# A fused recurrent attention and feed-forward kernel: a new written-out order and a new choice of engines for all its steps

## The chip, the cores and the metric

The kernel runs on one core of one Trainium2 chip. A core has five engines with queues of their own: TensorE (PE; its weight loads are shown as PEld), VectorE (DVE), ScalarE (ACT), GpSimd (POOL) and SyncE (SP), which here only issues DMA transfers. The metric is the device time of one execution in microseconds. Before the change, three runs took 184.97, 185.97 and 186.15, a median of 185.97.

## What is computed

Inputs are q, k, v and the logits of a gate f, each 4 x 8 x 768 x 48 (batch, heads, sequence, head width), and two weight matrices, 384 x 2048 and 2048 x 384. For each batch and head a 48 x 48 state runs along the sequence:

```python
f = 1.0 / (1.0 + np.exp(-f_logit))
for t in range(S):
    state = f[:, :, t, :, None] * state + np.einsum('bhd,bhe->bhde', k[:, :, t], v[:, :, t])
    y[:, :, t] = np.einsum('bhd,bhde->bhe', q[:, :, t], state)
# y as x: 3072 tokens x 384
h = x @ w_in
g = h * np.cos(h)
out = g @ w_out
```

## The kernel before

**Tiling.** The sequence is worked in 12 pairs of 128-position chunks: pair n is batch n // 3 and the 256 positions from 256 x (n % 3). Within a chunk the recurrence is written as masked attention; between chunks a state is carried. The feed-forward part works in 13 units of tokens (`UNITS`), the first two of 128 tokens (pair 0), the others of 256, one pair each: unit m is pair m - 1 from m = 2 on.

**Steps.** `describe` (L169 on) builds a graph of named steps. A name has a kind and a number, often a part: `sc5.1` is the scores of pair 5, half 1 (heads 4 to 7). The kinds, by engine:

- loads on SP: `f`, `k`, `q`, `v` of a pair (in halves for pairs 0 and 1), `w0.i` and `w1.i` for quarters of the two weight matrices, `out` for results;
- `zf` (L265): a matmul of a zero tile on TensorE, 128 x 512, whose result nobody reads; `ZEROS` says how many there are. `zsz`, `zqk`, `zvt`, `zsp` set buffers to zero;
- gate: `ex`, `ln`, `fx`, `fy` (ScalarE), `ad` (GpSimd), `cum` (TensorE, L375 and L381, running sums), `eb` and `ei` (ScalarE, decays up to a position and their inverse);
- `qa`, `ka`, `qm`, `km`: q and k times gate and decay, mostly on GpSimd; `vb` and the four `vt` copies of v; `wc` casts a quarter of the weights to bf16;
- `tq`, `tk`: transposes on TensorE (L436) for pairs 0 to 4, with the copy `qkt` out of PSUM; for pairs 5 to 11 `tq` is a transposing DMA of SP (L425);
- `sc` scores (L457), `am` their mask (VectorE), `ps` state updates (L480), `st` and `sz` carry and decay the state (VectorE; the last digit of the name tells the lower or the upper 64 partitions);
- `y` and `yi` (L532): output of a pair from within and from before the chunk, `xe` the copy to bf16;
- feed-forward: `h` (L580; six matmuls, or twelve in the first two units), `co` cosine (ScalarE), `g` the product (VectorE), `o` (L596; four matmuls, four such steps for 128 tokens), `ot` copy, `out`.

On TensorE, `h` and `o` use the whole array with 256 or 384 columns; `sc`, `ps`, `y` and `yi` are many small matmuls on parts of it.

**What sets the order.** There is no scheduler at build time. `ORDER` is a text in which every step stands with its engine (T, S, V, G, Y for PE, ACT, DVE, POOL, SP) and, where it writes a new buffer, the buffer's number. `emit` (L621) reads it from the front and gives each step's instructions to that engine. So the order of the words is the order of every queue, and a step that waits holds all that stand behind it on its engine. Semaphore waits follow from what steps read and write, and from buffers: a step that takes buffer 0 of a pool waits until the last reader of what was in it is done. Who made the text, a planner outside the kernel, isn't in the file; only its outcome is. A step may go to one of several engines, as listed at its `G.step`.

```python
    for word in ORDER.split():
        name, how = word.split(":")
        plan.append((G.steps[name], LETTER[how[0]], [int(x) for x in how[1:].split(",") if x]))
```

Of the kernel before, what the change touches and what calls it, by code (L numbers as in the profile page):

```python
# [15 lines left out]
B, H, S, D = 4, 8, 768, 48  # L16
# [16 lines left out]
ZEROS = 56  # L33
# [3 lines left out]
zsz.1:G zqk.1:G zsp.0:G f0.1:S0 f1.1:Y1 f0.0:S ex0.1:S f1.0:Y k0.1:Y0 q0.1:Y0 ex0.0:S k0.0:Y q0.0:Y  # L37
f3:Y2 ln0.1:S0 k1.1:Y1 k1.0:Y q1.0:Y1 fx0.1:S ex1.0:S ln0.0:S zf0:T0 zf1:T0 zf2:T0 zf3:T0 zf4:T0
zf5:T0 zf6:T0 zf7:T0 zf8:T0 zf9:T0 zf10:T0 zf11:T0 zf12:T0 zf13:T0 cum0.1:T0 zf14:T1 zf15:T1 zf16:T1
zf17:T1 cum0.0:T1 ei0.1:S0 fx0.0:S ei0.0:S eb0.0:S0 eb0.1:S ln1.0:S0 ex1.1:S ln1.1:S zf18:T2 zf19:T2  # L40
zf20:T2 zf21:T2 zf22:T2 zf23:T2 cum1.0:T0 ei1.0:S1 fx1.0:S zf24:T2 zf25:T2 zf26:T2 cum1.1:T1 zvt.1:G
zqk.0:G ka0.1:V zsz.3:V km0.1:V0 ka0.0:G qa0.1:V km0.0:V zsz.2:V qa0.0:V qm0.0:V ka1.0:G v0:Y0
vb0:G0 v1:Y1 f2:Y0 ex3:S eb1.0:S1 ln3:S0 fx1.1:S q1.1:Y zsp.2:V qm0.1:V w0.1:Y0 k3:Y0 tk0.1:T2
tk0.0:T3 tq0.0:T zf27:T4 tq0.1:T qkt0.0:V0 qa1.0:V qm1.0:V1 km1.0:V qkt0.1:V1 ad3:G0 vt0.3:S1
ei1.1:S zf28:T4 zf29:T4 zf30:T4 zf31:T4 zf32:T4 zf33:T4 zf34:T4 zf35:T4 zf36:T4 zf37:T4 zf38:T4
zf39:T4 zf40:T4 zf41:T4 zf42:T4 sc0.1:T2 eb1.1:S fy3:S fx3:S ex2:S ps0.0:T0,4 sc0.0:T6 am0.1:V0
am0.0:V1 w0.0:Y1 tk1.0:T5 cum3:T1 tq1.0:T qkt1.0:V2 ps0.1:T sz0.00:V2 sz0.01:V st0.10:V st0.11:V
q3:Y0 vt0.1:S ln2:S0 vt0.2:G zvt.0:G vt0.0:G vb1:G1 ka1.1:G km1.1:G ad2:G0 zf43:T2 zf44:T2 zf45:T2
# [141 lines left out]
def describe(nc, cpool, ppool, q, k, v, f_logit, moe_w_in, moe_w_out, out):  # L190
# [3 lines left out]
    def tl(shape, dt, name):  # L194
        return cpool.tile(shape, dt, name=name)
# [523 lines left out]
```

## Time and profile before

| | |
|---|---|
| profiled execution, us | 185.23 |
| its span, us | 183.5 |
| three runs, us | 184.97, 185.97, 186.15 |
| instructions | 5820 |
| busy: PE / PEld / DVE / ACT / POOL, us | 175.5 / 125.6 / 138.8 / 132.3 / 105.3 |
| matmuls | 2466, of which 56 are of zeros (15.8 us busy) |
| DMA | 33.92 MB, mean 185 GB/s |

The profile is of one execution on the chip. Times count from the start of its span. A row such as "54.12 0.53 issue" in the chain of waits is start, length and what the time was spent on; the chain is followed back from the last instruction to what released it. "issue" is time in which an engine waited for nothing that the profile shows. A row of groups has line, engine, operation, tiles written and read, count, then busy us, mean ns of one, and idle time of the engine before them with what ended it. A row of windows has the stretch, its length, and for each engine its busy time and in brackets the number of instructions, then the clock granted to TensorE, the busy share of the DMA engines and GB/s. Busy times of matmuls overlap a little, so prices of TensorE's steps are best taken from start to start in the chain.

### The profile page before, as it was taken

The page shows a single profiled execution, that of the slowest core. Times are in us where ns is not written, and L with a number is a line of the kernel's source. Part 1 is how long each engine was busy: PE and PEld are TensorE (multiplying, and loading weights), DVE is VectorE, ACT ScalarE, POOL GpSimd, SP SyncE. Part 2 cuts the span into 40 slices and gives each one's busy share as a digit, 9 for nine tenths or more (in the row PEclk, how much of TensorE's full clock was granted, in tenths as well). Part 3 has the DMA queues.
Part 4 walks back from the last instruction along what each step waited for, and adds up shares of the span by engine and source line. Part 5 has one row for each costly group of instructions (what it writes and reads, how often), then busy time and mean ns, then how long its engine had stood idle before and what let it go on. Part 6 is the DMA issues. An engine that isn't in the chain of part 4 may idle for free.

```text
span 183.5 us, 5820 instructions
## 1 busy us (share of the span) xinstructions
PE 175.5 (96%) x2466; PEld 125.6 (68%) x2466; DVE 138.8 (76%) x206; ACT 132.3 (72%) x192; POOL 105.3 (57%) x134
## 2 busy tenths in 40 slices
PE   7999889999989999999999999999999999999991
PEld 2455567976568866778667786667887677778650
DVE  5287998997578999995998887967797984573900
ACT  2786999874689999989999699767684436424520
POOL 7118599993779998999354896594996000000000
PEclk9999999999999999999999999999999999999999
DMA  5999999899997929979799949789743700030043
GB/s 141 261 261 284 345 345 338 264 282 310 249 265 163 297 42 194 302 81 217 101 230 270 259 95 212 166 240 255 154 78 106 151 4 4 0 129 4 0 172 129
DMA packets 72281, 33.92 MB, mean 185 GB/s; under 512 B 65344, under 2 KB 70720, under 8 KB 72256
## 3 DMA queue, kind: packets, MB, share of 16 engines
q1 hardware_dynamic: 71056, 33.07, 73.5%
q10 hardware_dynamic: 1200, 0.49, 1.1%
q8 instruction: 19, 0.31, 0.8%
q14 instruction: 6, 0.05, 0.1%
HBM read 25.17 MB, written 4.72 MB: 163 GB/s over the span
## 4 chain that ended last, share of the span: by engine, by line
PE 66%; DMA 8%; POOL 7%; ACT 7%; SPq 7%; issue 3%; DVE 0%; POOLq 0%; ACTq 0%
PE ps L580 29%; PE ps L596 28%; DMA f<-in_f_logit_dram 5%; POOL qk L405 4%; PE ps L532 4%; SPq L297 4%; DMA out_dram<-ot 2%; SPq L425 2%; PE ps L457 2%; PE ps L436 2%; POOL vt L198 1%; PE ps L480 1%; ACT vt L198 1%; POOL q L342 1%; ACT ls L334 1%
## 5 line engine op out<-in xcount | busy, mean ns | idle before, releaser
L562 DVE TENSOR_TENSOR g<-ps,co 128x1024 bf16<-128x1024 f32 x48 | 60.9, 1311 | 11.9 <-ACT co L585 11.7
L596 PE MATMUL ps<-w_out_bf,g 128*128 128x384 bf16 x384 | 69.1, 326 | 0.0
L580 PE MATMUL ps<-x,w_in_bf 128*128 128x256 bf16 (+1 forms) x624 | 68.3, 264 | 0.7 <-issue 0.3
L585 ACT ACTIVATE co<-ps,halfpi 128x1024 bf16<-128x1024 f32 x48 | 52.4, 1115 | 22.2 <-PE ps L580 20.1
L580 PEld LDWEIGHTS <-w_in_bf 128*128 128x128 bf16 x624 | 56.7, 98 | 10.3 <-issue 1.2
L596 PEld LDWEIGHTS <-g 128*128 128x128 bf16 x384 | 36.1, 98 | 21.1
L462 DVE TENSOR_TENSOR am<-ps,pmask 128x1024 bf16<-128x1024 f32 x24 | 28.8, 1219 | 5.2 <-PE ps L457 5.0
L405 POOL TENSOR_TENSOR qk<-k,bi 128x384 bf16<-128x384 f32 x21 | 20.9, 1003 | 0.9
L405 POOL TENSOR_TENSOR qk<-q,b 128x384 bf16<-128x384 f32 x20 | 19.8, 1003 | 0.7
L352 POOL TENSOR_TENSOR k<-k,f 128x384 f32<-128x384 f32 (+1 forms) x13 | 11.9, 916 | 12.8 <-ACT f L348 5.2
L265 PE MATMUL ps<-zero 128*128 128x512 bf16 x56 | 15.8, 428 | 1.5 <-DVE zero L204 1.2
L364 POOL TENSOR_TENSOR sp<-ls 128x384 bf16<-128x384 f32 x10 | 10.0, 1001 | 11.0 <-ACT ls L334 10.4
L198 POOL COPY vt<-vb 64x384 bf16<-64x384 bf16 x29 | 14.5, 503 | 2.5 <-issue 1.1
L504 DVE TENSOR_TENSOR sz<-ps,b 64x192 bf16<-64x192 f32 x40 | 14.0, 353 | 2.4 <-PE ps L480 1.1
L330 ACT ACTIVATE f<-f 128x768 f32<-128x768 f32 (+1 forms) x14 | 10.3, 747 | 6.2 <-DMA f<-in_f_logit_dram 6.2
L198 DVE COPY ot<-ps 128x384 f32<-128x384 f32 (+1 forms) x12 | 6.2, 522 | 11.3 <-PE ps L596 10.9
L198 ACT COPY ot<-ps 128x384 f32<-128x384 f32 (+1 forms) x14 | 6.2, 456 | 10.7 <-PE ps L596 7.6
L498 DVE TENSOR_TENSOR ps<-ps,sz 64x192 f32<-64x192 f32 x32 | 11.7, 366 | 1.5 <-PE ps L480 0.6
L198 ACT COPY vt<-vb 64x384 bf16<-64x384 bf16 x19 | 9.7, 508 | 2.7 <-POOL vb L198 2.5
L265 PEld LDWEIGHTS <-zero 128*128 128x128 bf16 x56 | 5.5, 107 | 8.0 <-issue 3.4
L342 POOL TENSOR_TENSOR q<-f,q 128x384 f32<-128x384 f32 x10 | 10.0, 1002 | 0.9 <-DMA q<-in_q_dram 0.9
L198 POOL CAST vb<-v 128x768 bf16<-128x768 f32 x9 | 7.4, 825 | 4.8 <-DMA v<-in_v_dram 4.8
(61 smaller groups left out, 169.2 us busy)
## 6 DMA issues: line engine op xcount, KB each, us to landing
v<-in_v_dram SPq DMA_DIRECT2D x12, 384.0 KB, 5.6
out_dram<-ot SPq DMA_DIRECT2D x22, 192.0 KB, 2.1
f<-in_f_logit_dram SPq DMA_DIRECT2D x10, 384.0 KB, 5.7
k<-in_k_dram SPq DMA_DIRECT2D x10, 384.0 KB, 6.0
q<-in_q_dram SPq DMA_DIRECT2D x10, 384.0 KB, 5.6
g<-in_moe_w_in_dram SPq DMA_DIRECT2D x4, 768.0 KB, 9.1
g<-in_moe_w_out_dram SPq DMA_DIRECT2D x4, 768.0 KB, 8.4
k<-in_k_dram SPq DMA_DIRECT2D x4, 192.0 KB, 5.1
```

The source lines that it names most:

```text
L198: (nc.scalar.copy if e == "ACT" else eng(e).tensor_copy)(out=o, in_=i)
L265: G.step(f"zf{i}", ("PE",), lambda e, dump=dump: nc.tensor.matmul(dump.ap, lhsT=zero[:, 0:128], rhs=zero, start=True, stop=True), writes=[ ...
L342: eng(e).tensor_mul(out=w.ap[:, :, 0, :], in0=t.ap[:, :, 1, :], in1=w.ap[:, :, 0, :])
L352: eng(e).tensor_mul(out=w.ap[:, :, 0, :], in0=w.ap[:, :, 0, :], in1=t.ap[:, :, 0, :])
L405: G.step(f"{nm}{n}.{u}", ("POOL", "DVE") if cut else ("POOL",), lambda e, u=u, j=j, src=src, dec=dec: eng(e).tensor_mul(out=qkp[u][j].ap[: ...
L462: G.step(f"am{n}.{u}", ("DVE",), lambda e, u=u, sc=sc: nc.vector.tensor_mul(out=am[u].ap.rearrange("p r b n -> p (r b) n"), in0=sc.ap.rear ...
L498: nc.vector.tensor_add(out=view()[s], in0=view()[s], in1=S0.ap[s, :, r, :])
L504: eng(e).tensor_mul(out=new.ap[s, :, r, :].rearrange("p (u a) n -> p u a n", u=2), in0=view()[s].rearrange("p (u a) n -> p u a n", u=2), i ...
L562: nc.vector.tensor_mul(out=o.rearrange("p b (n e) -> p b e n", e=2), in0=ph.ap.rearrange("p (b e n) -> p b e n", e=2, n=64), in1=co.ap.rea ...
L580: nc.tensor.matmul(ph.ap[:, i * T:(i + 1) * T].rearrange("p (g t) -> p g t", t=C), lhsT=w_in_bf[:, kk, f0:f0 + 128], rhs=xa[:, :, kk, :], ...
L585: G.step(f"co{m}.{j}", ("ACT",), lambda e, ph=ph, co=co: nc.scalar.activation(out=co.ap, in_=ph.ap, func=AF.Sin, bias=halfpi), reads=[ph], ...
L596: nc.tensor.matmul(po.ap[:, 0:DM], lhsT=gT.ap[:, j, i * C:(i + 1) * C], rhs=w_out_bf[:, j, :], start=(po.first and j == 4 * s), stop=(po.f ...
```

## The change

All of `ORDER` is replaced: every engine's queue has a new order, some steps are on other engines, and buffers have other numbers. `ZEROS` goes from 56 to 50. Nothing else differs; the steps, their matmuls and what each reads and writes are the same. The new text is described as planned with late blocks of TensorE's instructions, and with operations from partition 64 up running alone.

The core of it, as a diff (those parts of both texts of which the prediction speaks):

```diff
-ZEROS = 56
+ZEROS = 50
...
-zsz.1:G zqk.1:G zsp.0:G f0.1:S0 f1.1:Y1 f0.0:S ex0.1:S f1.0:Y k0.1:Y0 q0.1:Y0 ex0.0:S k0.0:Y q0.0:Y
-f3:Y2 ln0.1:S0 k1.1:Y1 k1.0:Y q1.0:Y1 fx0.1:S ex1.0:S ln0.0:S zf0:T0 zf1:T0 zf2:T0 zf3:T0 zf4:T0
...
-q3:Y0 vt0.1:S ln2:S0 vt0.2:G zvt.0:G vt0.0:G vb1:G1 ka1.1:G km1.1:G ad2:G0 zf43:T2 zf44:T2 zf45:T2
-zf46:T2 zf47:T2 zf48:T2 zf49:T2 sc1.0:T6 fx2:S ei3:S0 eb3:S2 vt1.3:S0 fy2:S vt1.2:S wc0.1:S
-sz0.11:V3 sz0.10:V ka3:G km3.0:G0 wc0.0:G qa3:G w0.3:Y2 qm3.0:G w0.2:Y3 k2:Y1 w1.0:Y0 w1.2:Y4
...
-ps3.1:T am2.1:V3 ot2:V1 st2.01:V sz3.00:V3 o1.1:T o1.3:T o3.1:T cum4:T7 sz3.01:V sz2.01:V vt3.0:G
-vt2.2:G ei4:S1 vt2.0:G eb4:S0 y3:T4,5 yi3:T k4:Y1 y2:T0,1 yi2:T ad5:G0 xe3.0:V1 xe3.1:V xe2.0:V0
-st3.11:V cum5:T7 ot3:V2 ot1:V3 sz3.11:V1 st3.10:V sz3.10:V h4.11:T4 fx4:S fx5:S xe2.1:S h3.20:T0
...
-h6.31:T co6.3:S1 y6:T2,3 yi6:T yi7:T6,7 y7:T h6.01:T4 h6.00:T xe6.0:V0 xe7.0:V2 xe6.1:V xe7.1:V
...
-ps10.1:T2,3 ps10.0:T out10:Y q10:Y0 am9.0:V0 sc9.1:T6 o13.2:T ot13:S0 y8:T4,0 yi9:T1 yi8:T am9.1:V2
-st10.00:V y9:T5 sz10.00:V1 xe9.1:V0 st10.01:V sz10.01:V st10.10:V sz10.10:V0 xe8.1:S1 xe9.0:S ka11:G
...
-out23.0:Y out18:Y out15:Y ot20:S0 out17:Y out23.1:Y out20:Y ot21:S2 out21:Y ot22.1:V3 ot22.0:S
-out22.0:S out22.1:Y
...
+qkt1.0:S0 eb1.1:S ei1.1:S ex2:S v1:Y1 am0.0:V0 am0.1:V1 sc1.0:T2 cum3:T1 qa1.1:V zsz.1:V am1.0:V2
+st0.10:V ei3:S0 ln2:S1 vb1:S1 vt0.1:G ka1.1:G qm1.1:G vt0.0:G w0.0:Y0 w0.1:Y1 zf33:T5 zf34:T5
+zf35:T5 zf36:T5 zf37:T5 zf38:T5 zf39:T5 zf40:T5 zf41:T5 zf42:T5 zf43:T5 ps1.0:T5,2 k3:Y0 q3:Y0
+km1.1:G vt1.1:S2 fx2:S fx3:S y0:T3 zf44:T6 ps1.1:T tk1.1:T6 tq1.1:T ad2:G2 xe0.0:S0 vt1.3:G vt1.0:G
+wc0.0:S zf45:T7 cum2:T3 wc0.1:G sz0.10:V1 st0.11:V sz0.11:V eb2:S0 fy3:S vt1.2:S xe0.1:S eb3:S2
+ei2:S1 fy2:S ka3:G w0.3:Y2 st1.00:V sz1.00:V3 qkt1.1:V1 zf46:T7 zf47:T7 sc1.1:T6 st1.01:V sz1.01:V
+am1.1:V0 w0.2:Y3 k2:Y1 zf48:T4 zf49:T4 yi1:T5,4 km3.0:G1 w1.0:Y0 qa3:G qm3.0:G w1.2:Y1 v2:Y1 km3.1:G
+qm3.1:G q2:Y0 wc0.2:G ka2:G km2.1:G2 km2.0:G wc1.0:G wc1.2:G vb2:G1 vt2.3:G0 vt2.0:G qa2:G vt2.1:G
+qm2.1:G qm2.0:G y1:T h0.01:T6 h0.00:T st1.10:V xe1.1:V1 st1.11:V xe1.0:V sz1.11:V1 co0.0:S0 g0.0:V4
...
+am2.1:V1 ps3.0:T6,4 ps3.1:T sc2.0:T2 am2.0:V3 sz3.00:V2 sz3.01:V q4:Y0 k4:Y1 o2.3:T o3.3:T y2:T2,3
+yi2:T st3.11:V xe2.0:V1 xe2.1:V st3.10:V cum4:T6 ei4:S1 eb4:S0 fx5:S o0.1:T o1.1:T ad5:G2 yi3:T3
+y3:T2 o3.1:T cum5:T6 o2.1:T ei5:S0 eb5:S1 ot3:S0 sz3.10:V1 xe3.0:V0 xe3.1:V sz3.11:V ot1:V1 ot2:V2
...
+eb8:S1 ex10:S ot9:S1 h6.30:T2 am7.0:V3 y6:T5,6 yi6:T y7:T0,1 yi7:T xe6.0:V1 q8:Y0 ln10:S1 ot7:S2
+h6.31:T st7.10:V xe6.1:S xe7.0:V2 sz7.10:V1 xe7.1:V st7.11:V sz7.11:V h7.31:T4 h7.30:T h6.01:T0
...
+ei11:S1 ot11:S2 eb11:S2 ot13:S0 y8:T6,7 yi8:T ps10.1:T0,1 ps10.0:T tq9.1:Y1 xe8.0:S1 sc9.1:T4
+xe8.1:S h8.01:T2 st10.00:V h8.00:T h9.30:T6 am9.1:V0 sz10.00:V1 st10.01:V sz10.01:V y9:T4,5 yi9:T
...
+ot23.1:S ot20:S0 o22.0:T7 o22.1:T o22.3:T o22.2:T out23.1:Y out23.0:Y out21:Y out20:Y ot22.0:S2
+out22.0:S ot22.1:V out22.1:Y
```

By engine, VectorE gets 185 steps for 191, ScalarE 183 for 185, GpSimd 133 for 126. Among those that move: three `qkt` copies from VectorE to ScalarE; of the casts of weights `wc0.1` and `wc1.3` go from ScalarE to GpSimd, `wc0.0` and `wc1.1` the other way; `km1.0` and `qm1.1` go from VectorE to GpSimd, and `f0.1` from ScalarE's DMA queue to SP's; 14 `vt` copies go from ScalarE to GpSimd and 5 back; 8 `ot` copies go from VectorE to ScalarE and 2 back.

130 lines of the change are left out of this document (62 added, 68 removed).

## The prediction

> **What bounds the kernel now.** I read the page first: which engine is busiest, and at which clock.
>
> ```profile
> PE 175.5 (96%) x2466; PEld 125.6 (68%) x2466; DVE 138.8 (76%) x206; ACT 132.3 (72%) x192; POOL 105.3 (57%) x134
> ...
> PEclk9999999999999999999999999999999999999999
> ...
> q8 instruction: 19, 0.31, 0.8%
> ```
>
> TensorE is the bound, at full clock, and the change takes no matmul of the reference away. So only three things can move the end: filler matmuls, time in which TensorE stands, and the start and tail around it. The last row leads to the standing. Queue q8 carries 0.31 MB in 19 pieces, 16 KB each; 2466 matmuls and 2466 weight loads are 4932 instructions, about 260 for a piece. A piece is thus a block of some 128 load-and-matmul pairs of TensorE's program. Next the windows, cut at the ends of the waits that the chain calls "issue" (waiting for nothing that the profile shows):
>
> ```profile
> 0.00:21.85 21.85, 19.85 (x223) 10.20 (x223) 14.56 (x41) 15.18 (x34) 11.11 (x24) 1.00 1.09 253
> 21.85:28.60 6.75, 6.04 (x128) 4.49 (x128) 6.46 (x13) 6.61 (x10) 5.47 (x6) 1.00 1.09 350
> 28.60:54.60 26.00, 25.49 (x383) 18.99 (x384) 21.15 (x27) 19.00 (x23) 20.52 (x23) 1.00 1.06 282
> 54.60:102.30 47.70, 47.08 (x768) 35.49 (x768) 42.47 (x62) 45.41 (x66) 37.34 (x44) 1.00 0.87 193
> 102.30:126.00 23.70, 23.36 (x383) 17.00 (x383) 19.26 (x26) 18.40 (x28) 17.90 (x22) 1.00 0.84 196
> ```
>
> The second bracket is the weight loads: 128, 384, 768, 383 between one wait and the next, that is 1, 3, 6 and 3 times 128. These waits stand at the borders of blocks: TensorE ran out of program. The chain in order of time shows them, and the prices that the rest needs:
>
> ```profile
> 28.39 0.24 issue
> ...
> 42.85 0.67 PE ps L436 x12
> ...
> 49.96 0.37 PE ps L480 x32
> ...
> 52.62 1.50 PE ps L532 x91
> 54.12 0.53 issue
> ...
> 55.33 9.19 PE ps L580 x84
> ...
> 102.01 0.34 issue
> ...
> 120.31 0.57 PE ps L457 x32
> ...
> 123.61 0.76 PE ps L596 x4
> 124.37 1.34 PE ps L532 x87
> 125.71 0.34 issue
> ...
> 147.78 0.90 PE ps L532 x56
> ...
> 171.24 8.46 PE ps L596 x52
> 179.73 0.37 DVE ot L198
> 180.12 0.32 ACT ot L198
> ```
>
> Prices: an h step is six matmuls, 9.19/84 x 6 = 0.66; an o step four, 8.46/52 x 4 = 0.65; a transpose step 0.67/3 = 0.22; a state update (ps) 0.37/2 = 0.19; scores (sc) 0.57/2 = 0.29; the y and yi of a pair 0.90 for 56 pairs of instructions. An o step behind small matmuls takes 0.76: a change of kind costs 0.1. The small matmuls run through 56 pairs in the time of eight large ones, so a block full of them is used up before the next one is there. The three later waits each stand in or just behind y/yi (L532). The last 128 pairs before them are worth 3.9, 3.9 and 2.6 us at these prices and took 4.7, 4.6 and 3.1 (counted back in the order to 49.97, 97.76 and 122.96): 0.8 + 0.7 + 0.5 = 2.0 us, of which about 0.3 is changes of kind. **Block waits after 42.85: 1.7 us.**
>
> The start is bound by loads and by two casts of weights. From the list of waits, SP's timeline and the list of issues (last number: us from issue to landing):
>
> ```profile
> POOL w_out_bf L198 <- DMA g<-in_moe_w_out_dram: 0.8, 1, 0.8
> ...
> PEld L580 <- ACT w_in_bf L198: 0.3, 1, 0.3
> ...
> PEld L580 <- POOL w_in_bf L198: 0.2, 1, 0.2
> ```
> ```profile
> 14.03 0.71 SPq L283 DMA_DIRECT2D g<-in_moe_w_in_dram  x1
> ...
> 15.36 1.39 SPq L283 DMA_DIRECT2D g<-in_moe_w_in_dram  x1
> ```
> ```profile
> g<-in_moe_w_in_dram SPq DMA_DIRECT2D x1, 768.0 KB, 7.4
> ...
> g<-in_moe_w_in_dram SPq DMA_DIRECT2D x1, 768.0 KB, 9.6
> ```
>
> The two issue rows belong to 14.03 and 15.36: w0.1 lands at 14.0 + 7.4 = 21.4, w0.0 at 15.4 + 9.6 = 25.0. TensorE's first h steps wait for their casts, although fillers (below) keep it busy meanwhile.
>
> **The change, part by part.** Fillers, 56 to 50:
>
> ```profile
> 1.19 5.47 PE L265 MATMUL ps<-zero 128*128 128x512 bf16 x14 [1.19 <-DVE zero L204]
> ...
> 12.23 3.40 PE L265 MATMUL ps<-zero 128*128 128x512 bf16 x15
> ```
>
> Six fewer at 3.40/15 = 0.22 are 1.3 us of TensorE (0.4 each in the first 5 us). They are worth that only if nothing else holds the start. So I follow what does.
>
> SP now issues w0.0 and w0.1 back to back, and k3 only behind them. Ahead of the first weight stand the same loads in both kernels (f, k, q and v of pairs 0 and 1, f of 2 and 3), so it lands at about 21.4 as before; the second comes without k3's 384 KB ahead of it: at the 282 to 350 GB/s of the windows 1.1 to 1.4 us sooner than 25.0. I take 23.5 (bounds: 22.8, if both share what w0.1 alone had, and 25.0, if nothing is gained). The cast of w0.1 moves from ScalarE to GpSimd's queue, and there it stands **in front of** all of pairs 3 and 2. GpSimd's own work before it ends earlier, near 22 by the rows below, so its extra work there (km1.0 and qm1.1 at 1.0 each) is hidden by the wait for w0.1; if that cover were gone it would cost up to 1 us.
>
> ```profile
> 22.95 1.01 POOL L352 TENSOR_TENSOR k<-k,f 128x384 f32<-128x384 f32 x1 [1.91 <-DMA k<-in_k_dram]
> ...
> 39.08 1.96 POOL L405 TENSOR_TENSOR qk<-q,b 128x384 bf16<-128x384 f32 x2
> ```
> ```profile
> L405 POOL TENSOR_TENSOR qk<-k,bi 128x384 bf16<-128x384 f32 x4 | 4.0, 1002 | 0.2
> ...
> L198 POOL CAST w_in_bf<-g 128x1536 bf16<-128x1536 f32 x2 | 2.9, 1464 | 0.1
> ```
> ```profile
> L198 POOL COPY vt<-vb 64x384 bf16<-64x384 bf16 x29 | 14.5, 503 | 2.5 <-issue 1.1
> ...
> L198 POOL CAST vb<-v 128x768 bf16<-128x768 f32 x9 | 7.4, 825 | 4.8 <-DMA v<-in_v_dram 4.8
> ```
>
> Before, GpSimd went from ka3 (22.95) to the end of qm2.0 (41.04) in 18.1 us: 12 products at 1.0, four casts at 1.46, 0.3 of starts. After, from wc0.1 to qm2.0 there are the same 12 products and four casts, and vb2 (0.83) and three vt2 copies (1.5) put ahead of qm2: 20.5 us. From 23.5 that ends at 44.0. TensorE's transpose tq2.0 reads it; before, it ran as part of the row at 42.85, with GpSimd 1.7 ahead. TensorE itself gets to it at about 43.4 (first h at 23.5 + 1.5 = 25.0, then 16 h, 7 o, 7 transposes, 2 sc and 2 ps, 17.7 at the prices, 0.3 of changes of kind and a little waiting), so **GpSimd is the later one, and the fillers' 1.3 us is hidden behind it**. So are the early block waits, and three qkt copies that move from VectorE to ScalarE (no row shows that: 0.67 by VectorE's row, 1.12 by ScalarE's 128x1024 activation; I take 1.1):
>
> ```profile
> L585 ACT ACTIVATE co<-ps,halfpi 128x1024 bf16<-128x1024 f32 x48 | 52.4, 1115 | 22.2 <-PE ps L580 20.1
> ...
> L198 DVE COPY qkt<-ps 128x1024 bf16<-128x1024 bf16 x10 | 6.6, 674 | 1.0 <-PE ps L436 1.0
> ```
>
> The first two are read by scores of pairs 0 and 1, which by my count of the queues run before 17, so well ahead of 23.5; the third has seven TensorE steps, 2.8 us, before its reader. Without cover each costs up to 1.1.
>
> From there on I count against before, where 42.85 to the last matmul at 179.73 took 136.9:
> - Behind tq2.0 the new order has 89 o steps for 91, two transpose steps and two half state updates fewer, since it did them before: -1.3 - 0.4 - 0.2 = -1.9.
> - Small matmuls are entered from large ones 18 times instead of 15: +0.3.
> - Block waits. Borders lie 128 pairs apart, counted on from 21.88 with six pairs fewer, so I know where they fall. The y and yi of pairs 2 and 3, and of 8 and 9, now have o or h steps between them, and a border no longer cuts off those of 6 and 7 behind scores. The dense blocks are worth 5.3 (y2, y3), 4.8 (y6, y7) and 3.6 (y8, y9) instead of 3.9, 3.9, 2.6; all others over 6. Taking what they took before (4.7, 4.6, 3.1) as what a block needs, none waits: -1.7 (bounds: 0 gained, to all of it).
> - Waits for data, about 0.6 over this stretch before (what is left of 136.9 over the steps' prices and the block waits), I leave: bounds 0 to 2. One that may come is wc1.1: GpSimd waited 0.8 for its load, now ScalarE does, with ex5 and ln5 of pair 5 queued behind; their reader cum5 has y2, y3 and two o steps before it.
>
> On SP, q2 now shares a buffer with q3 and holds the queue until qm3.1 has read it, near 31; w1.3, f4, v3 and w1.1 stand behind. w1.3 waits anyway until GpSimd has cast w1.0, near 37, so this costs nothing. VectorE's order changes between the lower and upper 64 partitions 50 times in both kernels: nothing. In the tail the halves of the last tile change places (ScalarE first, then VectorE): 0.37 and 0.32 one after the other either way, 0.
>
> **Sum:** 44.0 + 0.2 (the row's start against its read) + 136.9 - 1.9 + 0.3 - 1.7 = 177.8, against 179.73: -1.9. Span 181.6, this execution 185.23 - 1.9 = 183.3. The three runs have a median of 185.97, 0.7 above that execution, and a mean of 185.7; from these I say **183.8**. About 1% (1.9) is what this measurement tells from nothing, so the forecast lies on that border.
>
> [...]
>
> **The rivals.**
> 1. *The block waits stay, under another name*: they belong to the dense runs themselves, and y and yi are still there 12 times. For: all stand in or at L532. Against: the multiples of 128. Then -1.9 + 1.7 = -0.2: 185.6. That is also the case in which the plan doesn't do what it says. Chance 0.2.
> 2. *Slower: blocks come later than I take.* The block from 21.85 to 28.60 took 6.75, while loads ran at 350 GB/s. If a block needs L in the middle, the three dense ones wait 3L - 13.6 together (5.3 + 4.8 + 3.6): at L = 5.1 the 1.9 gained is gone, at 5.8 it is 1% slower, at 6.75 it is over 6.6 more, 190 and above. For: the early row. Against: 4.7, 4.6, 3.1 later, where loads run at 193 to 282. I price it at L = 6: +4.4, 188.2. Chance 0.12.
> 3. *GpSimd stands longer for w0.1*: each us later is one us, since everything of pairs 3 and 2 is behind it. If w0.1 shares the queue with k3 and q3 and lands at 25 to 26.3: +1.5 to 2.8, 185.3 to 186.6. Decides from 25.4. Chance 0.1.
> 4. *w0.1 lands before 22.8*, as its twin did in 7.4 us: TensorE's own work from h0.01 is then the gate: 182.5. Chance 0.1.
>
> Forecast: 0.48. **How the numbers follow.** Of the forecast's 0.48 some 0.36 lies beyond 1%, with all of rival 4 and a little of rival 1: faster 0.48. Slower: rival 2 and a part of rival 3, and waits of an order that no row shows: 0.17. Same: 0.35. The forecast alone would run from 182.6 to 185; rival 4's end and rival 2's beginning set the range, 181.8 to 187.2.
>
> **What would show it.** Right: wc0.1 on GpSimd idle before it until about 23.5, qm2.0 ending near 44; "issue" pieces above 0.3 in the chain gone after 45; last matmul near 177.8; tail of 3.7. Wrong: issue waits at y2, yi6, y8 or y9; a load of w0.1 after 25; ScalarE or VectorE named as releaser of TensorE for more than 1 us together after 45.

## The result, and the profile after

The changed kernel takes **185.43 us**, the median of 21 runs (183.88 to 187.94); beside it the kernel before takes 186.03 (184.91 to 186.82, also 21). The ratio is 0.9953, with a 95% interval of 0.993 to 0.9976: half a per cent faster, less than the one per cent that I had called the least this measurement tells from nothing. I had forecast 183.8, 1.2% less than before. The profiled execution took 186.14 us with a span of 184.3; its last matmul ended at 180.6, where I had 177.8. (The ratios here and below leave out runs more than 1.5% above the fastest of the same kernel: three of these 21, but six of ten of one experiment, y9_earlier, whose median says more than its ratio.)

The page of the changed kernel, the rows that answer to those of before:

```profile
PE 174.1 (94%) x2457; PEld 124.5 (68%) x2460; DVE 135.0 (73%) x200; ACT 133.0 (72%) x191; POOL 108.2 (59%) x141
...
PEclk9999999999999999999999999998899999999999
...
q8 instruction: 19, 0.31, 0.7%
```

The program still comes in 19 pieces. But the clock row, which was nines throughout before, has two eights now. The chain of waits, in order of time, around that place (line numbers are one less than before; L531 is y and yi, L579 h, L595 o):

```profile
121.19 0.95 PE ps L531 x56
...
124.82 0.39 PE ps L531 x19
125.21 1.99 issue
127.20 0.90 PE ps L531 x25
128.10 1.40 PE ps L579 x6
129.49 1.94 PE ps L595 x8
```

The first row is y8 and yi8. Then y9 begins, runs through 19 pairs, and TensorE **stands for 1.99 us** in the middle of it, waiting for nothing that the profile shows. After it an h step takes 1.40 and two o steps 1.94; they cost 0.66 and 1.30 elsewhere. The windows say why. Columns: stretch, length, busy us and count of PE, PEld, DVE, ACT and POOL, then the granted clock, DMA share, GB/s:

```profile
125.21:127.20 1.99, 0.00 (x1) 0.01 (x2) 0.36 (x1) 1.06 (x3) 1.85 (x4) 1.00 1.13 315
127.26:130.67 3.41, 3.41 (x36) 2.16 (x37) 2.24 (x3) 1.14 (x2) 1.57 (x2) 0.50 0.84 150
130.70:180.60 49.90, 49.89 (x541) 36.48 (x539) 29.26 (x28) 23.93 (x31) 8.14 (x12) 1.00 0.23 54
```

Right behind the wait the granted clock is 0.50 for 3.41 us, then 1.00 again. In the profile of the kernel before there was none: its records of the clock begin at 5.82 with 1.00 and change first at 183.31, behind the last matmul. Mean granted clocks of the 21 runs tell how often it comes: a stretch of 3.41 us at half clock in a span of 184 makes 1 - 0.5 x 3.41 / 184 = 0.991.

| granted clock | runs | span, us | time, us |
|---|---|---|---|
| 0.998 to 1.0 | 7 | 182.1 to 183.0 | 183.9 to 184.8 |
| 0.991 | 11 | 182.7 to 184.5 | 184.4 to 186.3 |
| 0.977 to 0.982 | 3 | 185.5 to 186.2 | 187.2 to 187.9 |

Of 71 runs of the kernel before that were made beside the experiments, 3 were below 0.995. So two things took the gain away: a wait of about 2 us in y9, and in two runs of three a fall of the clock.

Elsewhere this execution went as forecast. GpSimd's timeline and TensorE's (start, length, engine, line, operation; the wait before it in brackets):

```profile
23.61 1.46 POOL L197 CAST w_in_bf<-g 128x1536 bf16<-128x1536 f32 x1 [1.49 <-DMA g<-in_moe_w_in_dram]
...
44.00 1.46 POOL L197 CAST w_out_bf<-g 128x1536 bf16<-128x1536 f32 x1
```
```profile
44.12 0.40 PE L435 MATMUL ps<-ident,qk 128*128 128x128 bf16 x4
```

wc0.1 waits for its load and starts at 23.61 (forecast 23.5); the cast of GpSimd that follows qm2.0 starts at 44.00 (forecast 44.0 for qm2.0's end); TensorE's tq2.0 starts at 44.12. Counted border to border in the trace's instructions, the dense block of y2 and y3 took 5.43 and that of y6 and y7 4.73, without a wait. The third, of y8 and y9, worth 3.56 at the prices of the prediction, took 5.79.

### The profile page after: what moved, and what is told of

Read it like the earlier page. It is cut to its first block, busy times and chain, and to the rows that moved or that the text cites. A ratio compares the mean times of both kernels' runs of the same rounds, so it can differ in the third digit from the quotient of the medians.

```text
span 184.3 us, 5805 instructions
## 1 busy us (share of the span) xinstructions
PE 174.1 (94%) x2457; PEld 124.5 (68%) x2460; DVE 135.0 (73%) x200; ACT 133.0 (72%) x191; POOL 108.2 (59%) x141
## 4 chain that ended last, share of the span: by engine, by line
PE 83%; SPq 4%; DMA 4%; DVE 3%; issue 2%; ACT 2%; DVEq 0%; ACTq 0%
PE ps L579 34%; PE ps L595 34%; PE ps L531 5%; SPq L296 4%; PE ps L456 3%; DMA f<-in_f_logit_dram 3%; PE ps L479 2%; PE ps L435 1%; PE ps L264 1%; PE ps L374 1%; DMA out_dram<-ot 1%; DVE am L461 1%; DVE x L197 1%; DVE ps L497 1%; ACT co L584 1%
## 5 line engine op out<-in xcount | busy, mean ns | idle before, releaser
L595 PE MATMUL ps<-w_out_bf,g 128*128 128x384 bf16 x384 | 69.5, 328 | 0.0
L579 PE MATMUL ps<-x,w_in_bf 128*128 128x256 bf16 (+1 forms) x624 | 68.2, 266 | 0.2 <-DVE x L197 0.2
L579 PEld LDWEIGHTS <-w_in_bf 128*128 128x128 bf16 x624 | 56.5, 98 | 8.7 <-issue 0.5
L595 PEld LDWEIGHTS <-g 128*128 128x128 bf16 x384 | 36.1, 98 | 22.2 <-issue 0.7
L404 POOL TENSOR_TENSOR qk<-k,bi 128x384 bf16<-128x384 f32 x22 | 21.7, 1000 | 0.6
L197 ACT COPY ot<-ps 128x384 f32<-128x384 f32 (+1 forms) x20 | 9.0, 467 | 17.5 <-PE ps L595 13.5
L404 POOL TENSOR_TENSOR qk<-q,b 128x384 bf16<-128x384 f32 x21 | 20.8, 999 | 0.8
L197 POOL COPY vt<-vb 64x384 bf16<-64x384 bf16 x38 | 19.0, 501 | 3.4 <-issue 1.6
L264 PE MATMUL ps<-zero 128*128 128x512 bf16 x47 | 13.7, 419 | 1.3 <-DVE zero L203 1.2
L531 PE MATMUL ps<-am,vt 128*32 128x128 bf16 x384 | 8.1, 222 | 2.6 <-issue 2.0
L456 PE MATMUL ps<-qkt 48*64 48x128 bf16 (+1 forms) x304 | 9.2, 219 | 1.3 <-ACT qkt L197 1.1
L456 PEld LDWEIGHTS <-qkt 48*64 48x64 bf16 (+1 forms) x304 | 5.9, 103 | 4.7 <-ACT qkt L197 1.8
L531 PEld LDWEIGHTS <-vt 128*32 128x32 bf16 x384 | 5.9, 97 | 4.3 <-issue 4.3
```

Source lines behind the costliest of these rows:

```text
L197: (nc.scalar.copy if e == "ACT" else eng(e).tensor_copy)(out=o, in_=i)
L264: G.step(f"zf{i}", ("PE",), lambda e, dump=dump: nc.tensor.matmul(dump.ap, lhsT=zero[:, 0:128], rhs=zero, start=True, stop=True), writes=[ ...
L404: G.step(f"{nm}{n}.{u}", ("POOL", "DVE") if cut else ("POOL",), lambda e, u=u, j=j, src=src, dec=dec: eng(e).tensor_mul(out=qkp[u][j].ap[: ...
L456: nc.tensor.matmul(o[t0:t1, r, 2 * a + g, :].rearrange("p (e n) -> p e n", e=2), lhsT=wide[s, t0 // 64, :] if turned else wide[s].rearrang ...
L531: nc.tensor.matmul(py[g].ap[32 * c:32 * c + 32, C * m:C * m + C], start=(py[g].first and (g, c) not in begun), stop=(py[g].final and left[ ...
L579: nc.tensor.matmul(ph.ap[:, i * T:(i + 1) * T].rearrange("p (g t) -> p g t", t=C), lhsT=w_in_bf[:, kk, f0:f0 + 128], rhs=xa[:, :, kk, :], ...
```

## The experiments

**Theory 1**: TensorE ran out of program in y9. Its block was not there because the transfer of that block was late, and the wait made the clock fall in some runs. **Rivals**: y9 waited for data or a buffer that comes at 127.2 whatever stands ahead (theory 2); a dense run of y and yi costs 2 us wherever it stands, as rival 1 of the prediction had it (theory 3). A question inside theory 1: the trace's records of transfers put the start of this block's fetch at 124.49, 3.09 us behind the border (crossed at 121.40 in y8). Is that because of loads in the same DMA engines (1a), or is it asked for late (1b)? In the diffs below, the lines of `ORDER` are cut down to the words around the place that changes; its line breaks carry nothing.

### The same kernel again

> The changed kernel, unchanged, for a second profile. Theory 1: the wait inside y9 is there again, 1.5 to 2.5 us, at the same instruction; spans near 182.5 belong to a full granted clock (1.0), spans of 183.6 to 184.5 to a clock of 0.991, that is one stretch at half clock. If instead a run with a full clock has no wait in y9, the wait itself varies and the clock is only its consequence.

Median 184.89, ratio 0.9944 (0.99 to 0.9987). TensorE's timeline at y9:

```profile
124.70 0.46 PE L531 MATMUL ps<-am,vt 128*32 128x128 bf16 x19
126.78 0.40 PE L531 MATMUL ps<-am,vt 128*32 128x128 bf16 x13 [1.62 <-issue]
```

The wait is at the same instruction, 19 pairs into y9, and shorter (1.62); this execution had a granted clock of 0.999 and a span of 182.3. So the wait is there at a full clock too, and **the half clock is a second cost on top of it**: from the end of the wait to the last matmul it took 51.8 here (126.8 to 178.6) and 53.4 in the first profile (127.2 to 180.6), 1.6 more with the same instructions. Five of ten runs were at full clock (spans 182.1 to 182.7), five were not (183.5 to 186.1).

### y9 later, y9 earlier

```diff
-y9:T4,5 yi9:T
...
-sz10.11:V0 xe9.0:S0 fy11:S xe9.1:V g8.0:V h9.31:T o14.1:T0
+sz10.11:V3 fy11:S g8.0:V h9.31:T o14.1:T0
...
-o14.2:T h8.31:T4 h8.30:T h10.10:T2 h10.11:T h9.21:T6 h9.20:T o14.0:T
+o14.2:T o14.0:T y9:T4,5 yi9:T xe9.0:S0 xe9.1:V h8.31:T2 h8.30:T h10.10:T4 h10.11:T h9.21:T6 h9.20:T
```

> The changed kernel with y9 and yi9 moved on TensorE from behind h9.30 to behind h9.31, o14.1, o14.2 and o14.0 (o14.0 brought forward; the copies xe9 follow; the two PSUM tiles that they meet change places from there on). Nothing is left out. The 128 pairs that end in y9 are then worth 3.56 + 0.66 + 3 x 0.65 - 0.2 = about 6.0 us instead of 3.6. Theory 1 (TensorE runs out of program in y9, its block needs about 5.8 us from border to border there): no issue wait above 0.3 in y9, no stretch of half clock, last matmul near 180.6 - 4.3 = 176.3, span about 180.0, time about 181.9 in every run. Theory 2 (y9 waits for something that comes at 127.2 whatever stands before it: a buffer or data): TensorE now reaches y9 at about 127.3, so it would not wait either, but then what stands behind it (h8.31, h10.10) should take the wait: no gain in the sum over 0.5, 184.5 to 185.5. Theory 3 (dense runs cost this wherever they stand): 185.4 as before.

Median 183.67, ratio 0.9879 (0.9828 to 0.993). The wait in y9 is gone, and theories 2 and 3 with it: nothing behind y9 took it over, and y8 to yi9 cost no more than their prices. The gain was about 1 at full clock (spans 181.3 to 181.6 against 182.1 to 183.0), not the 2 that I had expected. Half of the shortfall is a new wait that the edit made: o14.0, brought forward, stood for g8.0.

```profile
128.66 0.82 PE L595 MATMUL ps<-w_out_bf,g 128*128 128x384 bf16 x4 [0.59 <-DVE g L561]
```

Three of the six runs had a lower clock all the same, and the profile shows where: at the front. From the windows of y9_later:

```profile
16.78:20.19 3.41, 3.11 (x18) 1.49 (x20) 3.27 (x7) 3.34 (x8) 2.99 (x5) 0.50 1.05 359
```

The other way:

```diff
-xe8.1:S h8.01:T2 st10.00:V h8.00:T h9.30:T6 am9.1:V0 sz10.00:V1 st10.01:V sz10.01:V y9:T4,5 yi9:T
+xe8.1:S h8.01:T2 am9.1:V0 y9:T4,5 yi9:T st10.00:V h8.00:T h9.30:T6 sz10.00:V1 st10.01:V sz10.01:V
```

> The changed kernel with y9 and yi9 moved the other way, directly behind h8.01, before h8.00 and h9.30 (am9.1 on VectorE ahead of st10.00). Nothing is left out. The dense block is then worth 2.3 us instead of 3.6. Theory 1: the border behind it is reached 1.3 us sooner and the block still comes near 127, so TensorE stands about 3.3 to 3.5 us in all (some of it for am9.1), the clock falls in every run, last matmul 1.3 to 2 later than in the changed kernel: 186 to 188. Theory 2 (data or a buffer that y9 needs at 127.2): y9 waits longer and at its first matmul, not inside it. Theory 3 (the wait is a fixed price of a dense run): same time as the changed kernel, 184.4 to 186.3.

```profile
123.63 0.63 PE L531 MATMUL ps<-am,vt 128*32 128x128 bf16 x31 [0.62 <-DVE am L461]
126.51 0.23 PE L531 MATMUL ps<-am,vt 128*32 128x128 bf16 x1 [2.25 <-issue]
```

Median **188.63**. y9 waits 0.62 for its data at its first matmul, and then 2.25 more inside, now 31 pairs in: with h8.00 and h9.30 behind it, the border falls later in y9. The block still comes at 126.5. One run of ten had a full clock (span 183.2), three had one stretch at half (185.0 to 185.4), six had two (0.982; 186.7 to 187.4). By these spans a stretch costs **about 1.9 us**; that rests on a single run at full clock, and at which of two places (below) the stretches of the other runs stood isn't known.

### What makes the block late

```diff
 def load(name, val, src, b, c, h0, h1):
...
-out=val.ap.rearrange("p h e d -> p h (e d)"),
+out=val.ap[:, 0:n_of(name, h1 - h0)].rearrange("p h e d -> p h (e d)"),
...
+def n_of(name, n):
+    return 1 if name in ("q10", "v11", "k11", "q11") else n
```

> The changed kernel with the loads q10, v11, k11 and q11, which are issued between 119.8 and 124.7, cut to one head of eight each; the other seven eighths of these loads are left out, so pairs 10 and 11 work on old data, while all instructions of the engines stay. Theory 1a (the block is late because its transfer stands behind these loads in the same DMA engines): its fetch starts within about 1 us of the border instead of 3.1 us behind it, the wait in y9 falls from 2.0 to about 0 to 0.3, the clock does not fall: span about 180 to 180.7, 182 to 182.5. Theory 1b (the lag does not come from these loads: the fetch is asked for late): wait in y9 of about 2 as before, clock at half in about two of three runs, 184.4 to 186.3.

Median 183.14, ratio 0.9847 (0.9782 to 0.9911). TensorE's timeline, y8's row and y9's (the edit adds four lines, so L535 is y):

```profile
121.35 0.63 PE L535 MATMUL ps<-am,vt 128*32 128x128 bf16 x32
...
124.92 0.63 PE L535 MATMUL ps<-am,vt 128*32 128x128 bf16 x32
```

y9's 32 matmuls stand in one row, without a wait. The fetch started 0.72 us behind the border instead of 3.09, and the block took 3.54 from border to border, just its work of 3.56: it was there when needed. The profiled span was 180.7. So the loads made the block late (1a). That "the clock does not fall" did not come: two of the four runs had 0.988, without a wait in y9. This run left work out; the next one doesn't. The wait ahead of out13 on SyncE is used to hold the loads back:

```diff
-o14.1:T0 q10:Y1 v11:Y1 out13:Y k11:Y2
+o14.1:T0 out13:Y q10:Y1 v11:Y1 k11:Y2
```

> The changed kernel with one word moved on SyncE: out13 stands ahead of q10 instead of behind v11. Its tile is ready at about 121.5, so q10 and v11, which were issued at 119.8 and 120.5, are now issued at about 121.9 and 122.6, behind the moment at which TensorE crosses the border in y8 (121.35) and its next block is asked for. Nothing is left out, and TensorE's order is that of the changed kernel. Theory 1a (the block's transfer queues behind loads that were issued just before it): the fetch starts within 1 us of the border instead of 3, the wait in y9 falls from 1.6 to 2.0 to below 0.3; span 180.7 to 181.2 at a full clock, 182.4 to 182.9, unless the later q10 makes scores of pair 11 wait (up to 1). Theory 1b (the lag of 3 us belongs to the border, not to the loads ahead): wait in y9 as before, 184.1 to 186.

Median 184.66, ratio 0.99 (0.9863 to 0.9937). SyncE's timeline, then TensorE's, of out13_first:

```profile
123.20 0.33 SPq L606 DMA_DIRECT2D out_dram<-ot  x1
123.59 0.43 SPq L296 DMA_DIRECT2D q<-in_q_dram  x1
124.11 1.29 SPq L296 DMA_DIRECT2D v<-in_v_dram  x1
```
```profile
122.82 0.63 PE L531 MATMUL ps<-am,vt 128*32 128x128 bf16 x32
...
126.39 0.63 PE L531 MATMUL ps<-am,vt 128*32 128x128 bf16 x32
```

(This execution, with a mean clock of 0.991, had lost about 1.5 us at the front by a stretch at half clock, so all times are later: ten fillers at 18.41 took 3.49, in the second profile of the changed kernel 2.32.) With the same TensorE order as the changed kernel and one word moved on another engine's queue, y9 runs through: the border in y8 is crossed at 123.04, q10 is issued at 123.59, and the block took 3.54. The DMA view of the stretch from the border on (each digit is the busy share in a fortieth of the window) for the changed kernel from 121.40 to 124.45, just before its fetch, and for out13_first from 123.04 to 125.20:

```profile
DMA  4873923679999899999999999999999999999999
...
q1 hardware_dynamic: 1994, 0.78, 105.2%
```
```profile
DMA  0000000000000000093689999998946124436799
...
q8 instruction: 1, 0.02, 3.3%
```

In the changed kernel the engines are full with q1's packets from the tenth digit on, and there is no q8 row for 3 us. In out13_first they are idle behind the border, and the fetch (q8) is the first packet that comes, at 123.96, 0.92 us behind it. So 0.7 to 0.9 from border to start is the least seen at this place but for one profile (zeros_56, below), and TensorE runs from the block about 2.6 later; a dense block of 3.5 is just enough with idle DMA engines, and 2 too little behind two loads. In ten of the eleven profiles with the whole of q10 and v11 issued ahead of the border the fetch started 2.7 to 3.7 behind it; the eleventh is that of zeros_56.

At full clock out13_first has spans of 181.4 to 181.8, about 1 less than the changed kernel. That is less than the wait of 1.6 to 2.0; two new waits are listed in its trace behind 130, an o step's for a copy out of its bank (0.6) and scores' for VectorE's g (0.2). Five of its eight runs were below 0.995.

### Borders and fillers

```diff
-ZEROS = 50
+ZEROS = 56
...
-zf40:T5 zf41:T5 zf42:T5 zf43:T5 ps1.0:T5,2
+zf40:T5 zf41:T5 zf42:T5 zf43:T5 zf44:T5 zf45:T5 zf46:T5 zf47:T5 zf48:T5 zf49:T5 ps1.0:T5,2
```

> The changed kernel with six more fillers of zeros behind zf43, 56 instead of 50, so that every later border of 128 pairs comes six pairs earlier in the order. Nothing is left out. Two questions. Where the wait stands: if it belongs to the border (theory 1), it moves from 19 matmuls into y9 to 13 matmuls into y9, about 2 us as before; if it belongs to y9's data or to y9 itself, it stays at 19 or is ahead of the first. Whether six fillers are hidden, as the prediction had it for the step from 56 to 50: then tq2.0 starts at 43.8 to 44.3 as before and the time is that of the changed kernel (184.4 at a full clock, 186 with a stretch at half); if they are not, tq2.0 starts up to 1.3 later, less the 0.3 to 0.6 that TensorE stands for vb1 there.

Median 185.36, ratio 0.991 (0.9872 to 0.9949). Rows of its timeline, tq2.0 and y9:

```profile
44.83 0.39 PE L436 MATMUL ps<-ident,qk 128*128 128x128 bf16 x4
...
126.03 0.63 PE L532 MATMUL ps<-am,vt 128*32 128x128 bf16 x32
```

Neither expectation on y9 came: in this execution there is no wait in it at all. The fetch started 0.95 us *ahead* of the border, at 121.0, between q10 (issued at 120.5) and v11 (121.2); so it was ahead of most of what stands in its way otherwise. Why six pairs do that, and four (zeros_front, below) don't, I can't tell. Six runs of ten were at 0.991; where the clock fell in them, no profile shows. On the fillers: tq2.0 starts at 44.83. Of the seven executions with 50 fillers and no early fall of the clock six have 43.8 to 44.2, but vt2_behind (below) has 44.76; the three with 54 fillers have 44.0 to 44.5. So up to 0.7 of the 1.3 us of six fillers may show here, and one execution can't tell it from that spread.

```diff
-vb2:G1 vt2.3:G0 vt2.0:G qa2:G vt2.1:G qm2.1:G qm2.0:G
+vb2:G1 qa2:G qm2.1:G qm2.0:G vt2.3:G0 vt2.0:G vt2.1:G
```

> The kernel of y9_later_g8 with three copies of GpSimd, vt2.3, vt2.0 and vt2.1, moved from ahead of qm2.1 and qm2.0 to behind them. Nothing is left out. If GpSimd's chain behind w0.1 sets the time of tq2.0, as the prediction had it, qm2.0 ends 1.5 sooner and tq2.0 starts sooner by what TensorE has in hand, 0.3 to 0.7, and the time falls by as much against y9_later_g8. If TensorE itself is the gate by now (theory 1 of the second profile: qm2.0 ended 0.6 ahead of tq2.0), qm2.0 ends near 42.0, tq2.0 stays within 0.2 of 44.2 and the time is that of y9_later_g8.

Median 185.4, ratio 0.9964 (0.9935 to 0.9994); y9_later_g8, its own base, had 184.84. From the waits, GpSimd's timeline (qm2.1 and qm2.0) and TensorE's (tq2.0):

```profile
PE ps L479 <- ACT vb L197: 0.9, 1, 0.9
```
```profile
41.29 1.96 POOL L404 TENSOR_TENSOR qk<-q,b 128x384 bf16<-128x384 f32 x2
```
```profile
44.76 0.39 PE L435 MATMUL ps<-ident,qk 128*128 128x128 bf16 x4
```

qm2.0 ends at 43.25, 1.5 ahead of tq2.0, and tq2.0 is no sooner; it is later, because ps1.0 waited 0.9 for ScalarE's cast of v1 at the front of this execution. In the profile of y9_later_g8 too qm2.0 had ended (43.61) ahead of tq2.0 (43.98). GpSimd isn't the gate in these two.

### The versions with y9 later

```diff
-sz10.00:V1 st10.01:V sz10.01:V st10.11:V co8.0:S2 sz10.11:V3 fy11:S g8.0:V
+sz10.00:V1 st10.01:V g8.0:V sz10.01:V st10.11:V sz10.11:V3 fy11:S
```

> The kernel of y9_later with g8.0 earlier on VectorE (behind st10.01, ahead of sz10.01, st10.11 and sz10.11) and co8.0 ahead of am9.1 in the text. Nothing is left out. In y9_later TensorE no longer stood in y9, but 0.6 us ahead of o14.0, for g8.0. Theory 1: this wait goes too, no idle time of TensorE above 0.2 after 35; at a full granted clock a span of 180.7 to 181.0 (the 181.3 to 181.6 of y9_later less 0.6), 182.4 to 182.8; with a stretch of half clock in the first 25 us, as y9_later had in three of six runs, 0.8 to 1.1 more. Theory 3 (a dense run costs its 2 us wherever it stands): the wait comes back in or behind y9, 183.3 to 184.4.

```profile
PE ps L595 <- DVE sz L503: 1.8, 1, 1.8
```

Median 184.84, ratio 0.9938 (0.9909 to 0.9968): **worse than y9_later**, and by my own mistake, not by theory 3. o14.1 writes the PSUM bank that sz10.01 reads. With g8.0 ahead of sz10.01, and g8.0 waiting for its cosine, TensorE stood 1.8 us for VectorE two steps sooner than it had before. The next run puts g8.0 behind sz10.01:

```diff
-sz10.00:V1 st10.01:V g8.0:V sz10.01:V st10.11:V
+sz10.00:V1 st10.01:V sz10.01:V g8.0:V st10.11:V
```

> The kernel of y9_later with g8.0 on VectorE one place group earlier: behind sz10.01, ahead of st10.11 and sz10.11, not ahead of sz10.01 as in y9_later_g8, where o14.1 stood 1.8 us for sz10.01 because it takes the PSUM bank that sz10.01 reads. Nothing is left out. Theory 1: g8.0 ends at about 126.7, as TensorE gets to o14.0; neither the 0.6 of y9_later nor the 1.8 of y9_later_g8 is left: no idle time of TensorE above 0.3 behind 35, span 180.7 to 181.0 at a full clock, 182.4 to 182.8; 0.8 to 1.1 more with an early stretch at half clock, as in three of six runs of y9_later. Theory 3 (a dense run of y and yi costs 2 us wherever it stands): 184.1 or more.

Median 183.43, ratio 0.9865 (0.9836 to 0.9893). Neither wait is left, but the spans at full clock, 181.2 to 181.6, are those of y9_later, not 0.6 less. What was saved at 128 was lost again by 152: between two borders there, 144.8 to 151.9, TensorE took 7.10, where y9_later took 6.70, and 0.2 of that is a wait of scores for VectorE's g. Half of the runs were below 0.995 again.

For that, two fillers ahead of sc1.0, where TensorE had stood 1.1 us in every profile, and two behind zf43; and buffer 1 for ot22.0, which waited for a transfer out of buffer 2 at the end. First on y9_later_g8, then on y9_later_v, then alone on the changed kernel (without the buffer):

```diff
-ZEROS = 50
+ZEROS = 54
...
-am0.0:V0 am0.1:V1 sc1.0:T2
+am0.0:V0 am0.1:V1 zf33:T2 zf34:T2 sc1.0:T2
...
-ot22.0:S2
+ot22.0:S1
```

> The kernel of y9_later_g8 with four more fillers where TensorE stood in the first 21 us (two ahead of sc1.0, where it waited 1.1, and two behind zf43, where it waited 0.6), so 54, and with buffer 1 instead of 2 for ot22.0, which waited 0.4 for a transfer out of buffer 2 to land. Nothing is left out. Theory 1 (the clock falls after TensorE has stood, the early stretch at half clock comes from the waits of 1.1, 0.6 and 0.25 there): fewer runs below 0.995 in granted clock than in y9_later_g8, tail 3.4 instead of 3.7 us, span 180.3 to 180.7 at a full clock, 182.0 to 182.4. If the early stretch does not come from these waits, it is there as often; if the fillers are not hidden, 0.4 to 0.9 is lost at the front.

Median 184.34, ratio 0.9904 (0.9866 to 0.9941), with the 1.8 of y9_later_g8 still in it, so its name is not earned. But all six runs had a granted clock of 0.998 or more, against six of twelve of y9_later_g8 at 0.997 or more.

> The kernel of y9_later_v with the four fillers and the buffer for ot22.0 of the run called best (54 fillers; ot22.0 in buffer 1). Nothing is left out. If the early stretch at half clock comes from TensorE's standing in the first 21 us, all runs have a granted clock above 0.995, as the six runs of best had; tail 3.4; span 180.3 to 180.9, 182.0 to 182.6, the fastest version. If not, half of the runs are 0.8 to 1.1 longer. A risk: the borders are four pairs earlier than in y9_later_v, and o14.0 or y9 may meet a late block again: up to 1.

Median **182.88**, ratio **0.9837 (0.9807 to 0.9867)**: the fastest version, 1.6% faster than before by the ratio, and 1.1 to 1.4% below the two medians of the changed kernel. All six runs had a clock of 0.997 or more. The expected 182.0 to 182.6 was not quite reached. The end of its chain:

```profile
169.73 7.81 PE ps L595 x48
...
177.57 0.33 ACT ot L197
...
177.92 0.36 DVE ot L197
```

The last matmul ends at 177.5, and the tail is 3.4 for 3.7. That 0.3 is the buffer's; what is left of the gain over y9_later_v goes with the fillers.

> The changed kernel with the same four fillers alone (two ahead of sc1.0, two behind zf43; 54). Nothing is left out. It tells the two places apart at which the clock can fall. If the runs of the changed kernel at 0.991 fell at the front, where TensorE stood 1.1 and 0.3 to 0.6, these fillers end them: all runs above 0.995, span 182.0 to 182.7 or less. If they fell behind the wait in y9, as in the first profile (127.3), about half of the runs stay at 0.991 with spans of 183.5 to 184.5. The borders come four pairs earlier, so the wait in y9 may be shorter, as with 56 fillers.

Median 185.29, ratio 0.9959 (0.9924 to 0.9995). Four of ten runs stayed below 0.995, and the profile is one of them. Its windows:

```profile
125.59:127.76 2.17, 0.00 (x0) 0.00 (x0) 0.38 (x2) 0.33 (x1) 2.03 (x4) 1.00 1.12 319
128.73:132.14 3.41, 3.41 (x14) 1.85 (x13) 3.31 (x5) 2.04 (x3) 1.65 (x3) 0.50 0.76 113
```

The wait in y9 is there (2.17), and the clock falls behind it. So the clock has two places at which it falls: the wait in y9, seen in two profiles, and the front, seen in those of y9_later and out13_first, whose front is that of the changed kernel. The four fillers cure the front (no fall in 12 runs of best and y9_later_vz; 13 in the 24 runs of y9_later, y9_later_v, out13_first and light_loads, which have no wait in y9 but lack these fillers), and not the fall behind y9.

## Why the prediction was wrong, by its own steps

- **Block waits: the step that failed.** "Taking what they took before (4.7, 4.6, 3.1) as what a block needs, none waits: -1.7." For y2/y3 and y6/y7 that held. For y8/y9 the need was 5.8 (5.4 to 6.0 where TensorE stood), not 3.1. The 3.1 was no property of the place but of what SyncE had issued just before. SyncE's timeline in the kernel before, where the border was crossed at 122.96 and the fetch started at 123.67, and in the changed kernel, border 121.40, fetch 124.49:

```profile
119.99 2.05 SPq L607 DMA_DIRECT2D out_dram<-ot  x4
122.09 0.45 SPq L297 DMA_DIRECT2D k<-in_k_dram  x1
123.48 0.33 SPq L607 DMA_DIRECT2D out_dram<-ot  x1
123.86 1.86 SPq L297 DMA_DIRECT2D q<-in_q_dram  x2
```
```profile
119.81 0.58 SPq L296 DMA_DIRECT2D q<-in_q_dram  x1
120.50 0.57 SPq L296 DMA_DIRECT2D v<-in_v_dram  x1
121.57 1.09 SPq L606 DMA_DIRECT2D out_dram<-ot  x1
```

  Before, the loads of q were issued at 123.86, behind the fetch; one load, k11's, stood 0.9 ahead of the border, behind four results. After, q10 and v11 were issued 1.6 and 0.9 ahead of the border, and the fetch came only behind packets of theirs. That the engines are busy does not tell the two apart. In the kernel before, from 119.9 to the start of the fetch at 123.67:

```profile
DMA  5999999999999999999999999899999996998934
...
q1 hardware_dynamic: 1669, 1.06, 100.2%
```

  They were as full, with the results, k11 and a transposing DMA, until shortly ahead of the fetch, which still came 0.7 behind the border. So a busy share alone doesn't tell how long a fetch waits; what differs is which transfers were issued, and when. I had followed SyncE's queue at the start and past q2, and had not asked what it issues beside the three dense blocks. The wait of 0.5 at this place was to go; it became 2.0 by the chain, 2.2 by the blocks (5.79 less 3.56).
- **The clock was no term of the sum at all.** I had read "full clock" from the page of before and kept it. A fall behind y9 cost 1.6 us between the two profiles of the changed kernel (about 1.9 by the spans of y9_earlier), and one at the front 0.5 to 1.6 (median spans with and without: y9_later_v 182.1 and 181.6, y9_later 182.6 and 181.5, out13_first 183.0 and 181.4); two runs of three had one or more.
- **The rest of the sum was right, and 0.9 too high.** light_loads has the same order without the wait: tq2.0 at 44.24, last matmul at 176.9, 132.7 us; my sum had 44.2 to 177.8, 133.6. The data waits of 0.6 that I had left in are gone: no wait of TensorE is listed in its trace from 44 to 178. The remaining 0.3 I can't divide between changes of kind and prices. So without the late block the forecast would have erred on the other side: 182.5 at full clock.
- **The sum, put right**: 183.3 for a full clock, less 0.9, plus the wait of 1.6 to 2.0, is 184.0 to 184.4; the seven runs at full clock have a median of 184.4. Most of the other fourteen lie above, and the median of all is 185.4.
- **The front.** The landing of w0.1, the start of wc0.1 and the time of tq2.0 were right to 0.2. That "GpSimd is the later one" was not: in the first profile and in light_loads it is by 0.1, in y9_later_v both come to tq2.0 together, and in the others TensorE gets to it 0.3 to 1.5 behind qm2.0 (1.8 to 1.9 after an early fall of the clock). What holds it, the waits name only in part: v1's cast (0.3 to 0.9 in five profiles). So the cover for the fillers' 1.3 us was not there as I had it; what taking six away was worth is not shown (at most about 0.7 by zeros_56).
- **The copies qkt on ScalarE** were hidden from the end, as said. But the first scores of pair 1 stood 1.1 for one, and it is in this neighbourhood that the clock falls at the front. A wait that costs nothing by the chain cost 0.5 to 1.6 in about half of the runs by the clock.
- **The rivals.** Rival 1 named the time (185.6) but not the cause: out13_first, y9_later and light_loads run the same dense steps without a wait. Rival 2, blocks that come later than taken, is what happened, in one place of three: 5.8 - 3.6 = 2.2 for 3L - 13.6. Rivals 3 and 4, w0.1 sooner or later, did not occur (wc0.1 began between 23.0 and 23.9 in all profiles). Of the signs I had named, "issue waits at ... y9" was the one that told.

Not tried: the old order with only its y and yi moved apart, so what the first two block waits were worth by themselves rests on the trace (0.53 and 0.34 before, nothing after).

## What to carry to other kernels

A long unrolled program is itself a load, and here it came behind the others (its fetch started 3.09 us behind the border with two loads ahead, 0.92 with idle engines): where a run of small instructions uses up a block faster than a fetch takes, look at what the DMA queues are given just ahead of the border, not only at the instructions. A wait can cost more than its length: in some executions 1.4 to 2.2 us of standing were followed by 3.4 us at half clock, in others not. Fillers over such waits can pay even where the chain says that the waits cost nothing; over those at the front here they took the falls from 13 of 24 runs to none of 12. And a need measured at the old place holds only with what the old place had beside it, here one load just ahead of the border and not two.

## What the runs showed of the hardware

- The start of a block's fetch lies on both sides of the border. In the profile of the kernel before it runs from about 2.1 us ahead (fetch at 138.11, border at 140.26) to 4.2 behind (32.80, border at 28.60). Where TensorE stood for a block, it ran 2.4 to 2.7 us after the start of the fetch (before: 26.11 to 28.60, 123.67 to 126.05; first profile: 124.49 to 127.20). q8 carries just these 19 pieces, and still the fetch for y9 started 3.09 us behind the border, with q1's loads in the engines.
- Changes of the granted clock lie a multiple of 3.41 us apart in the profiles of both kernels. In the first profile of the changed one the trace's records of the clock begin at 4.38 and change at 127.26, 130.67 and 185.29, which is 36, 37 and 53 times 3.413 later; in that of the kernel before, 5.82 and 183.31 are 52 times 3.413 apart. In the first profile and in zeros_front the whole wait (1.99 and 2.17) lies within the 3.41 us that end with the fall (123.85 to 127.26 and 125.32 to 128.73). In y9_earlier's profile (mean clock 1.0) the clock did not fall after 2.25; nor did it for 1.62 (again, 0.999) or 1.8 (y9_later_g8 1.0, best and vt2_behind 0.999). At the front of y9_later it fell at 16.78, where TensorE had stood 0.33 and 1.10 with only small matmuls between; in again the same two waits, with the same matmuls between, had no fall behind them. So the length of a wait alone does not decide it. That its place between two multiples of 3.41 does is an estimate of mine from the spacing and from these two falls, not tested by itself. TensorE's busy time in the 3.41 us that end with a fall was 1.42 in the first profile and 2.0 in y9_later (13.37 to 16.78, small matmuls).
